# Longer score visits, an earlier first pair and fewer DMA turns in a fused cosine-attention and expert kernel

## The chip, the cores and the metric

The kernel runs on one core of a Trainium2 chip. The metric is the device time of one execution in microseconds (us); less is better. The core's engines are named as in the profile: PE (TensorE, matmuls; PEld is its weight load), ACT (ScalarE), DVE (VectorE), POOL (GpSimd) and SP (SyncE, which here only issues DMAs). ACT and POOL issue a few DMAs as well.

## The reference

For each of 8 batches and 12 heads there are q, k and v of 448 tokens by 64. The rows of q and k are divided by their norms, the scores are divided by tau = 0.1, a softmax follows, and its product with v is the attention output. The 12 heads side by side make x of 3584 tokens by 768, and two matmuls with a gate stand behind it.

```
q_n = q / (norm(q) + 1e-6);  k_n = k / (norm(k) + 1e-6)
attn = softmax(q_n @ k_n.T / tau)            # per batch and head
x = (attn @ v).transpose(0, 2, 1, 3).reshape(3584, 768)
h = x @ w_in                                 # 768 x 2048
out = (h * cos(h)) @ w_out                   # 2048 x 768
```

## The kernel before

**Names.** A pair g is two heads of one batch: there are 48 pairs, six to a batch. A unit u is three pairs (six heads, half a batch): 16 units. q, k and v of a unit are loaded as fp32 into `raw` and `vin`, which have two buffers each, used by even and by odd units. The 448 tokens are held as 4 chunks of 112. W1 is `w_in`, loaded in two halves, W2 is `w_out`, loaded in four quarters; both are fp32 in memory and bf16 on the chip, and are loaded by POOL's queue.

**The norms of a unit** (`norms`): `square` makes the squares (POOL, some on ACT or DVE), `reduce` sums them on DVE (L700), `rnorm` makes the inverse root with two ACT instructions, logarithm (L708) and exponential (L711), and `scale` multiplies, mostly on POOL (L719), into bf16 `qks`.

**Turning.** `transposes(g)` makes `qkT` of a pair. Below `BYPE` = 9 it is done by PE (L745) into the PSUM bank `PO2` (called TP there) with a copy by DVE; from pair 9 on it is a transposing DMA on SP's queue (L734).

**Scores and softmax.** `scores(g, c)` is one chunk: two matmuls (two heads, each on 64 rows of the array, side by side) into one of two PSUM buffers, SC0 and SC1 (L762), followed by one ACT exponential over 896 columns into `PX` (L767). PE goes to the scores of two chunks at a time, a "visit": `both`, called twice per pair. A score matmul uses 64 rows of the array and every other matmul the full 128, and changing from one to the other costs PE time. The planner calls this modes R and F.

**Values.** `attend(g)` is 32 small matmuls into the PSUM buffer AV (L785), then on DVE the reciprocal of the row sums (L794) and the scaling into `xs` (L795). `xs` is turned to `xT` by a DMA, or for the pairs of the first batch and the last pair of every batch by PE (L809) into the AV buffer.

**The two matmuls of a batch.** `m1(b)` is 96 matmuls (L826) in eight groups over the buffers SC0, SC1 and AV, each group followed by a cosine on ACT (L840, a sine with a shifted input) and a product on DVE (L842). ACT loads another function table before the cosines and loads the first one again after them (L618). `m2_add` and `m2_emit` make the second matmul (L877), in half tiles of 16 matmuls in `PO` and `PO2`; these are stream "B", the filler that PE takes between visits. Each half tile is copied out by DVE (L884).

**Order.** Each engine works through a fixed list in order. The lists are made when the kernel is built: operations are recorded in program order, and `arrange` plays them against listed costs and picks an order for every engine (`play`, `pick`). Up to the first `m1` PE's order is free in a window; afterwards PE takes the groups of stream "A" in order, and stream "B" between them. Gaps of the plan get dummy matmuls (L919, "filler"). In the main loop, `pair(g)` issues the first visit, `attend(g - 1)`, the DMA turn of pair g + 3 and the second visit; `m1(b)` stands after pair 12 for batch 1 and one pair into the next batch for the others (`LAG`).

Of the kernel before, what the change touches and what calls it, by code (L numbers as in the profile page):

```python
# [6 lines left out]
ACT = mybir.ActivationFunctionType  # L7
# [7 lines left out]
    "sq": ["AD", "A", "P", "P", "P", "P"],  # L15
# [4 lines left out]
DEBUG = 0  # L20
PACE, AHEAD = 0.97, 9.5
# [7 lines left out]
class Program:  # L29
# [11 lines left out]
    PATIENCE = 0.25  # L41
# [56 lines left out]
    def share(self, start, jobs, factor=1.0, first=1.2):  # L98
# [3 lines left out]
        came = {o.idx: start[o.idx] + first + (0.5 if e == "POOL" else -0.1) for e in jobs for o in jobs[e]}  # L102
# [69 lines left out]
    TRIALS = [(m, h, k) for m in ((0.0, 1.0), (0.3, 1.1), (0.8, 1.1)) for h in (0.1, 0.2) for k in (0.05, 0.2)]  # L172
# [3 lines left out]
    def arrange(self):  # L176
# [12 lines left out]
        for self.margin, self.hold, self.look in self.TRIALS:  # L189
            nominal, self.lands = first, {}  # L190
            for n in range(self.PASSES):
# [14 lines left out]
                if n:  # L206
                    spans = [self.rehearse(f, x) for f, x in self.STAGE]
                    if DEBUG:
                        print(self.margin, self.hold, self.look, n, "%.1f" % self.span, ["%.1f" % x for x in spans])
# [8 lines left out]
    def play(self):  # L218
# [45 lines left out]
        def pick():  # L264
# [4 lines left out]
            if groups and groups[0][0].free:  # L269
                for grp in groups[: self.WINDOW]:  # L270
# [3 lines left out]
                    if left[o.idx] == 0:  # L274
                        t = max(free["PE"], ready_at[o.idx])
                        if s is None or t < s - self.PATIENCE:
                            s, c = t, (t, o, grp)
                return c
            for grp in groups[:3]:
                t = when(grp)  # L280
                if t is not None and (s is None or switched(t, grp[0]) < s - self.PATIENCE):
                    s, c = switched(t, grp[0]), (t, grp[0], grp)
            if fill and left[fill[0].idx] == 0:
                o = fill[0]
                t = max(free["PE"], ready_at[o.idx])
# [16 lines left out]
        def transfer(upto):  # L302

            while clock[0] < upto:
# [10 lines left out]
                for h in run:  # L315
                    h[2] -= step * h[0].pkt / turn
                    if h[2] <= 1e-9:
                        o = queue[h[0].eng].pop(0)[0]
                        o.end = max(clock[0] + self.LAST, o.start + o.cost + 1.0)
                        if o.start > 5.0:  # L320
                            o.end += self.margin[0] + (self.margin[1] - 1.0) * (o.end - o.start)
# [8 lines left out]
        while todo or any(queue.values()):  # L330
# [23 lines left out]
            if e == "PE":  # L354
                if current:
                    current.pop(0)
                elif grp is fill:
                    fill.pop(0)
# [15 lines left out]
            if o.dma is not None:  # L374
                queue[e].append([o, o.start + (1.7 if e == "POOL" else 1.1), o.bulk + 0.02])
# [110 lines left out]
def bass_cosine_attention__then__act_gcu_kernel(  # L486
# [25 lines left out]
    BYPE = 9  # L512
# [5 lines left out]
    NO = 4  # L518
    DEFER = (2 * PB,)
# [58 lines left out]
    POv = PO.ap().bitcast(BF16)  # L578
    vav = [t.ap().rearrange("p (x d) -> p x d", d=DV) for t in va]
# [9 lines left out]
    XTv = AV.ap().bitcast(BF16)  # L589
# [48 lines left out]
    for i in range(2):  # L638
        pool(lambda e, i=i: e.memset(vav[i][:, :, D : D + 1], 1.0), (), [("va", i)], 0.15, label="ones")
# [7 lines left out]
    def load(u, p0, p1, apart=False):  # L647
        i = u % 2
        h = slice(2 * p0, 2 * p1)
        f = [lambda e, x=x, t=t: e.dma_start(  # L650
            rawv[i][:, h, NJ * x : NJ * x + NJ, :].rearrange("p h s d -> p h (s d)"), src(t, u, 2 * p0, 2 * (p1 - p0)))
            for x, t in enumerate((k, q))]
        for x in ((0,), (1,)) if apart else ((0, 1),):
            eng = "ACT" if u in HALF and x == (1,) else "SP"
            behind = quick[-1] if eng == "ACT" and quick else None if eng == "ACT" or not loads else loads[-1]
            dma(eng, [f[y] for y in x], (), [("raw", i, p, y) for p in range(p0, p1) for y in x],
                "raw%d_%d_%s%s" % (i, p0, x, eng), 0.95 * (p1 - p0) * len(x), "load u%d p%d" % (u, p0), behind, 0.068)
# [421 lines left out]
```

## Time and profile before

| | |
|---|---|
| runs | 434.74 us median of 5 (433.13 to 436.41) |
| profiled execution | 433.13 us, of which the span from first to last instruction is 431.2 us |
| granted clock of PE | 1.00 |
| PE busy | 418.1 us (97%), 3756 matmuls |
| ACT / DVE / POOL busy | 264.5 / 213.2 / 192.3 us |
| HBM | 45.61 MB read, 11.01 MB written |

The stages on PE, from its timeline (us from the start of the span): scores of batch 0 to 37, its first matmul `m1(0)` to 57, the pairs of batch 1 to 91, `m1(1)` to 109.6, then one batch after another. `m1(3)`, `m1(4)`, `m1(5)` and `m1(6)` begin at 192.5, 240.3, 288.1 and 335.8. `m1(7)` ends at 395.2, and what is left of the second matmul runs to 427.8. A line of the profile names engine, source line, operation and tiles; "idle ... <-" says what ended the engine's idle time. A filler matmul (L919) counts as busy. The width of a busy PE says little, since it is busy nearly always: the places to look at are the starts of instructions, and what stands between them.

### The profile page before, as it was taken

To read this page: it belongs to the slowest core of one execution; us is meant where nothing else is said; L and a number is where in the kernel's file an instruction comes from. 1 tells how busy PE (TensorE), PEld (TensorE's weight loads), DVE (VectorE), ACT (ScalarE), POOL (GpSimd) and SP (SyncE) were. 2 spreads that over 40 slices of the span, in tenths; PEclk is the share of its full clock that TensorE was granted. 3 is DMA by queue.
4 is the path that set the end of the run, shared out by engine and by line. 5 is a ranking of instruction groups with operands and counts; after the bars stand their busy time and mean duration, and the time that the engine had idled before them with its cause. 6 is when DMAs were issued, how large, how long until landed. Compare 5 with 4: busy or idle time off the path is not lost.

```text
span 431.2 us, 8767 instructions
## 1 busy us (share of the span) xinstructions
PE 418.1 (97%) x3756; PEld 225.7 (52%) x3756; DVE 213.2 (49%) x297; ACT 264.5 (61%) x319; POOL 192.3 (45%) x118
## 2 busy tenths in 40 slices
PE   7889989999999999999999999999999999999996
PEld 3445535554555545555555545555555545555663
DVE  5776655465636356434853375425853343344221
ACT  3887476974877647774677648774777547734000
POOL 2995248923676546932496057913596000000000
PEclk9999999999999999999999999999999999999999
DMA  8999999998179596648656692649647102200322
GB/s 218 246 242 211 241 245 199 160 249 216 33 175 248 105 273 183 114 112 239 168 117 119 164 285 62 113 128 241 149 109 133 49 0 59 59 2 2 102 79 77
DMA packets 94631, 63.87 MB, mean 148 GB/s; under 512 B 55040, under 2 KB 89600, under 8 KB 94592
## 3 DMA queue, kind: packets, MB, share of 16 engines
q1 hardware_dynamic: 90064, 56.16, 55.9%
q0 software_dynamic: 3680, 6.29, 7.9%
q10 hardware_dynamic: 848, 0.86, 0.7%
q8 instruction: 30, 0.49, 0.5%
q14 instruction: 9, 0.07, 0.1%
HBM read 45.61 MB, written 11.01 MB: 131 GB/s over the span
## 4 chain that ended last, share of the span: by engine, by line
PE 79%; DMA 7%; ACT 7%; POOL 4%; issue 1%; DVE 1%; SPq 1%; ACTq 0%
PE PO L877 26%; PE SC L826 20%; PE AV L826 12%; PE AV L785 9%; PE SC L762 8%; ACT PX L767 5%; DMA raw<-in_q_dram 4%; POOL qks L719 3%; PE SC L877 2%; DMA vin<-in_v_dram 2%; POOL sq L693 1%; DMA qkT<-qks 1%; PE AV L877 1%; ACT L618 1%; PE PO L745 0%
## 5 line engine op out<-in xcount | busy, mean ns | idle before, releaser
L767 ACT ACTIVATE PX<-SC 112x896 bf16<-112x896 f32 x192 | 164.9, 914 | 43.8 <-PE SC L762 43.4
L877 PE MATMUL PO<-W,gT 128*128 128x384 bf16 x816 | 148.6, 326 | 0.0
L693 POOL TENSOR_TENSOR sq<-raw 112x1024 bf16<-112x1024 f32 x42 | 78.9, 1895 | 99.2 <-DMA raw<-in_q_dram 99.1
L877 PEld LDWEIGHTS PO<-W,gT 128*128 128x128 bf16 x816 | 73.0, 97 | 56.9 <-issue 13.0
L719 POOL TENSOR_TENSOR qks<-raw,rn 112x1024 bf16<-112x1024 f32 x47 | 88.4, 1903 | 27.8 <-ACT rn L711 27.8
L826 PE MATMUL SC<-xT,W 128*128 128x448 bf16 x480 | 95.5, 352 | 0.3 <-ACT PX L767 0.3
L842 DVE TENSOR_TENSOR gT<-SC,cosb 128x896 bf16<-128x896 f32 x40 | 43.6, 1091 | 55.2 <-ACT cosb L840 54.7
L840 ACT ACTIVATE cosb<-SC,cst 128x896 f32<-128x896 f32 x40 | 40.2, 1007 | 48.5 <-PE SC L826 46.1
L826 PEld LDWEIGHTS SC<-xT,W 128*128 128x128 bf16 x480 | 46.6, 98 | 43.2 <-issue 0.7
L700 DVE TENSOR_REDUCE n<-sq 112x16 f32<-112x1024 bf16 (+1 forms) x49 | 58.1, 1191 | 14.6 <-POOL sq L693 9.3
L826 PE MATMUL AV<-xT,W 128*128 128x448 bf16 x288 | 58.7, 352 | 1.0 <-DVE gT L842 0.4
L762 PE MATMUL SC<-qkT 64*128 64x448 bf16 x384 | 55.3, 355 | 4.1 <-ACT PX L767 2.2
L785 PEld LDWEIGHTS AV<-va,PX 112*128 112x128 bf16 x1536 | 49.4, 97 | 15.5 <-issue 11.5
L785 PE MATMUL AV<-va,PX 112*128 112x65 bf16 x1536 | 54.7, 193 | 0.8 <-ACT PX L767 0.8
L884 DVE COPY osb<-PO 128x384 f32<-128x384 f32 x51 | 28.2, 553 | 38.0 <-PE PO L877 38.0
L840 ACT ACTIVATE cosb<-AV,cst 128x896 f32<-128x896 f32 x24 | 24.2, 1008 | 32.6 <-PE AV L826 32.4
L794 DVE RECIPROCAL rcp<-AV 112x8 f32<-112x8 f32 x48 | 9.9, 207 | 66.1 <-PE AV L785 66.1
L826 PEld LDWEIGHTS AV<-xT,W 128*128 128x128 bf16 x288 | 27.5, 98 | 28.7 <-issue 3.8
L842 DVE TENSOR_TENSOR gT<-AV,cosb 128x896 bf16<-128x896 f32 x24 | 26.2, 1091 | 19.0 <-ACT cosb L840 18.8
L795 DVE TENSOR_TENSOR xs<-AV,rcp 112x512 bf16<-112x512 f32 x48 | 33.2, 691 | 2.0
L762 PEld LDWEIGHTS SC<-qkT 64*128 64x128 bf16 x384 | 13.2, 94 | 36.5 <-ACT PX L767 17.4
L667 POOL CAST va<-vin 112x1536 bf16<-112x1536 f32 x14 | 20.5, 1466 | 10.0 <-DMA vin<-in_v_dram 7.1
(34 smaller groups left out, 122.5 us busy)
## 6 DMA issues: line engine op xcount, KB each, us to landing
vin<-in_v_dram SPq DMA_DIRECT2D x16, 672.0 KB, 9.5
raw<-in_k_dram SPq DMA_DIRECT2D x12, 672.0 KB, 8.1
raw<-in_q_dram SPq DMA_DIRECT2D x12, 672.0 KB, 10.0
W<-in_moe_w_in_dram POOLq DMA_DIRECT2D x2, 1536.0 KB, 15.6
W<-in_moe_w_out_dram POOLq DMA_DIRECT2D x4, 768.0 KB, 22.4
raw<-in_k_dram SPq DMA_DIRECT2D x12, 224.0 KB, 7.7
out_dram<-osb SPq DMA_DIRECT2D x7, 336.0 KB, 2.8
out_dram<-osb SPq DMA_DIRECT2D x8, 288.0 KB, 2.7
```

Source lines behind the costliest of these rows:

```text
L693: pool(lambda e, x=x, y=y: e.tensor_tensor(y, x, x, ALU.mult), src_, dst, 0.1 + n * 1.78e-3, label="sq%d.%d" % (u, p))
L700: dve(lambda e, w=w: e.tensor_reduce(out=n2v[i][:, 2 * p : 2 * p + 2, w], in_=sqv[p][:, :, w, :], axis=mybir.AxisListType.X, op=ALU.add), ...
L719: f = lambda e, s0=s0, s1=s1: e.tensor_tensor(qksv[i][:, p, s0:s1, :, :].rearrange("p s h d -> p h s d"), rawv[i][:, h, s0:s1, :], bass.AP ...
L762: t = e.matmul(SCv[z][:, a, 0:S], qkT[k].ap()[r, NP * c : NP * c + 128], qkT[k].ap()[r, S : 2 * S], start=True, stop=True)
L767: act(lambda e: e.activation(PXv[j][:, c, 0 : 2 * S].rearrange("p (a s) -> p a s", a=2), SCv[z][0:NP, :, 0:S], ACT.Exp, scale=1.0 / TAU), ...
L785: t = e.matmul(AVv[:, a, DV * x : DV * x + n], PXv[j][:, c, k : k + 128], vav[i][:, NJ * (2 * p + a) + c, 0:n], start=(c == 0), stop=(c == ...
L795: dve(lambda e: e.tensor_tensor(xsv[y].rearrange("p x h d -> p h x d"), AXv[:, :, :, 0:D], bass.AP(rcp[y], 0, [[NS, NP], [NJ, 2], [1, NJ], ...
L826: t = e.matmul(ph[:, a, 0:S], W1v[:, c, 128 * n : 128 * n + 128], xTv[b % 2][:, c, :], start=(c == 0), stop=(c == NKC - 1))
L840: act(lambda e, ph=ph, cz=cz: e.activation(cosv[cz], ph[:, :, 0:S], ACT.Sin, bias=cst.ap()[:, 0:1], scale=1.0), names(gi) + ["cst0"], [("c ...
L842: dve(lambda e, ph=ph, cz=cz, gi=gi: e.tensor_tensor(gTv[:, 2 * gi : 2 * gi + 2, S * (b % 2) : S * (b % 2) + S], ph[:, :, 0:S], cosv[cz], ...
L877: r = e.matmul(po[:, 0:HW], gTv[:, y, col : col + 128], W2v[:, y, HW * hf : HW * hf + HW], start=(y == 0), stop=(y == NF - 1))
L884: dve(lambda e, po=po, o=o, hf=hf: e.tensor_copy(osb[o].ap()[:, HW * hf : HW * hf + HW], po[:, 0:HW]), keys, [("osb", o, hf)], HW, label=" ...
```

## The change

1. **Three-chunk visits.** From pair `G3` = 12 on, three pairs are handled as four visits of three chunks each, where they were six visits of two. The three chunks go to the AV buffer, SC0 and SC1 in turn. So the AV buffer is shared by scores, `attend` and `m1`, and the PE turn of `xs` moves from it to `PO` or `PO2`. `m1(b)` stands after the second visit of a batch, with the first two visits' `attend` ahead of it.
2. **First pair by head.** The load of pair 0 is cut into four DMAs of one head each (two on SP, two on ACT); squares and sums of this pair are made by head, and the sums of k and q in one reduce.
3. **Early AV in four pieces.** Up to `m1(0)`, `attend` is four groups of eight matmuls that PE can place singly, where it was two of sixteen. The DVE copy of v is cut in three.
4. **Turns.** `BYPE` = 12: pairs 9 to 11 are turned by PE where they went by DMA; pairs 8 to 11 go into the AV buffer, between the visits of batch 1.
5. **W1.** Both halves are issued by POOL right behind the square of pair 2, one after the other. Before, the first waited for v of unit 0, and the second stood seven POOL instructions later, ahead of W2.
6. **Other moves.** The squares of pair 3 go from POOL to ACT; unit 2 gets its norms as two pairs and one, and its last square goes from ACT to POOL. The load of unit 5 waits in order for the turn of pair 12. The second matmul's half tiles are kept and spread by `KEEP` and `SPREAD`, so that a part of each batch stands right behind `m1`. The planner's listed costs for DMAs and its trial settings are other ones.

```diff
-    "sq": ["AD", "A", "P", "P", "P", "P"],
+    "sq": ["AD", "A", "P", "A", "P", "P"],
...
-    BYPE = 9
+    BYPE = 12
+    GATE = "T12"
+    BEHIND = "sq0.2"
+    G3 = 12
+    KEEP = (0, 1, 0, 1, 0, 1, 0)
+    SPREAD = (5, 6, 6, 6, 6, 6, 6)
+    AT, AT1 = 1, 1
...
     def load(u, p0, p1, apart=False):
+        if u == 0 and p0 == 0:
+            for a in range(2):
+                for x, t in enumerate((k, q)):
+                    eng, past = ("SP", loads) if x == 0 else ("ACT", quick)
+                    dma(eng, [...src(t, u, a, 1)], (), [("raw", i, 0, x, a)], ...)
...
+        if g >= PB + UP - 1:
+            views, keys = (AVt, AVt), ("AV", "AV")
...
     def scores(g, c):
-        j, k, z = g % 2, g % UH, (c + 1) % 2
+        j, k, q = g % 2, g % UH, NJ * g + c
+        name, bank = PHs[1 + (c + 1) % 2 if g < G3 else q % 3]
...
+        step = 1 if P.free else 2
+        for x0 in range(0, NJ, step):
+            P.op("PE", lambda e, x0=x0: av(e, x0, step), ...)
...
+        keys, view = ["PO"], POv
+        if g >= 2 * PB - 1:
+            keys, view = [(["PO"], POv), ([("TP", 0), ("TP", 1)], TPv)][nhalf[0] % 2]
...
+    def visit(g, n):
+        q = NJ * g + 3 * n
+        for x in range(q, q + 3):
+            scores(x // NJ, x % NJ)
...
+    def project(b, g):
+        m1(b)
+        if g in DEFER:
+            norms(g // UP + 1, 0)
+            for x in range(g + 3, g + 4 + AT1):
+                transposes(x)
+        ...                      # loads of units 2b + 4 and 2b + 5, after m1's first matmul
+        m2_add(b)
+        m2_emit(SPREAD[b])
...
     load_w1(0)
-    after(P.ops[-1], find("load v u0"))
     load_w1(1)
...
+    P.order_only(find("sq0.2"), find("W1.0"))
+    P.order_only(find(BEHIND), find("W1.1"))
...
-    for g in range(PB, NG):
-        pair(g)
-        if g in points:
-            m1(points[g])
-            ...
+    for g in range(G3, NG, 3):
+        for n in range(4):
+            if n < 3:
+                ahead(g + n)
+            grouped(visit, g, n)
+            if n < 3 and g + n > PB:
+                attend(g + n - 1)
+            if n == 0:
+                values(g)
+            if g % PB == 0 and g > PB and n == (AT if g > 2 * PB else AT1):
+                project(g // PB - 1, g)
```

## The prediction

> **What bounds the kernel now.** I read the page first, then the table by stage, the timeline of one steady batch, the chain, and the DMA queues of the early stage. The table's columns are the stretch, its length, then busy us and number of instructions for PE, PEld, DVE, ACT and POOL, PE's clock, DMA share and GB/s.
>
> ```profile
> PE 418.1 (97%) x3756; PEld 225.7 (52%) x3756; DVE 213.2 (49%) x297; ACT 264.5 (61%) x319; POOL 192.3 (45%) x118
> ```
>
> ```profile
> 57.00:91.10 34.10, 32.32 (x355) 17.39 (x355) 18.02 (x27) 28.16 (x36) 26.16 (x15) 1.00 1.04 202
> ...
> 240.30:288.10 47.80, 47.69 (x442) 25.59 (x441) 24.73 (x34) 32.18 (x39) 25.32 (x14) 1.00 0.64 154
> ```
>
> PE is the bound, at full clock, from 109 us on; no other engine passes 70% of a steady batch (second row). In the first row (pairs of batch 1) ACT is at 28.2 of 34.1 us and the DMA engines are full: that stage is a near tie. One steady pair in PE's timeline, then the ACT and DVE of the same pair:
>
> ```profile
> 215.69 2.12 PE L877 MATMUL PO<-W,gT 128*128 128x384 bf16 x12
> 217.74 0.55 PE L762 MATMUL SC<-qkT 64*128 64x448 bf16 x4
> 218.23 1.14 PE L785 MATMUL AV<-va,PX 112*128 112x65 bf16 x32
> 219.20 0.81 PE L877 MATMUL PO<-W,gT 128*128 128x384 bf16 x4
> 219.95 0.55 PE L762 MATMUL SC<-qkT 64*128 64x448 bf16 x4
> ```
>
> ```profile
> 218.15 1.73 ACT L767 ACTIVATE PX<-SC 112x896 bf16<-112x896 f32 x2 [0.78 <-PE SC L762]
> ...
> 219.40 0.21 DVE L794 RECIPROCAL rcp<-AV 112x8 f32<-112x8 f32 x1 [2.22 <-PE AV L785]
> ...
> 219.64 0.69 DVE L795 TENSOR_TENSOR xs<-AV,rcp 112x512 bf16<-112x512 f32 x1
> ```
>
> Read starts, not ends. In the chain, 24 matmuls of m1 take 4.54 us (at 192.69), 0.189 each, and in the tail 32 of the second matmul take 5.20, 0.1625 each. A visit of two chunks lasts from 217.74 to 218.23 = 0.49; two chunks are 0.38, so leaving the 64-row mode costs 0.11. Twelve L877 matmuls are 1.95, but 215.69 to 217.74 is 2.05: entering costs 0.10. **A visit costs 0.21 us beside its work.** The 32 AV matmuls take 0.97. A steady batch is then 96 x 0.189 + 0.27 (one wait for DVE in m1) + 100 x 0.1625 + 12 x (0.38 + 0.21) + 6 x 0.97 + 0.2 (the turn L809) = 47.7; from m1(4) to m1(5) it is 47.8. Nothing else is in it.
>
> The chain that ended last:
>
> ```profile
> 57.45 1.01 ACT cosb L840
> 58.48 1.28 ACT L618
> 59.77 2.54 ACT PX L767 x3
> ...
> 70.06 5.30 DMA qkT<-qks
> ...
> 156.62 1.90 POOL sq L693
> ...
> 420.04 5.20 PE SC L877 x32
> ```
>
> Early it is ACT, not PE: exponentials to 35.9, last cosine and table to 59.77; then one turn that sits 5.3 us behind loads on SP. From 192.69 on it is PE without a break.
>
> **The change part by part.** The sum is made against the profiled execution (span 431.2, time 433.13; the 1.9 us around the span stay). That run is the fastest of the five: the median lies 1.6 above, and I carry the difference over to it.
>
> *Three-chunk visits.* The built order of the changed kernel shows them from pair 12 on. From m1(1) to the end there were 69 visits of two chunks and are 46 of three (34.5 pairs both times). Saved: 23 x 0.21 = **4.8**.
>
> What this adds is a wait. Before, 12 filler matmuls or a whole visit lay between the last exponential of a pair and its AV. The new order is visit, 4 or 8 L877, AV, and the AV needs a chunk of the visit just made. The first exponential starts 0.41 after its visit (217.74 to 218.15), takes 0.914 (page, L767), a second follows 0.82 later (1.73 for two), and PE sees the end some 0.05 later (in the early rows a score started at 11.15, the exponential before it ended at 11.10). A three-chunk visit lasts 3 x 0.189 + 0.11 = 0.67.
> - First and second AV of three: visit and 4 matmuls, 1.32, against 0.41 + 0.91 + 0.05 = 1.37: wait 0.05.
> - Third: second chunk needed, 0.67 + 1.30 = 1.97 against 2.19: wait 0.22.
> - Last pair: third chunk, 2.62 against 3.01: 0.4.
>
> Per three pairs 0.32; 35 AVs are left: 11.7 x 0.32 + 0.4 = **4.1 given back**. Here a rule speaks harder: the Trainium skill, "TensorEngine Tiling (Array Packing)", section "PSUM Bottleneck", says that tiling the array speeds up the matmuls but not the emptying of PSUM, which may then be the bound. Taken whole (each AV waits for the visit's three exponentials, 3.01 after its start) the cost is some 1.7 a pair on two AVs of three and 1.0 on the third, over 50 in all. By the rows only the chunk that the AV reads counts, and ACT has 15 us free per batch; I take the rows.
>
> The AV buffer is now handed from AV to DVE to the next visit. L794 starts 0.20 after the AV matmuls and L795 ends 1.13 after them; 8 L877 and the entry are 1.40. Hidden, by 0.2 us. A sum L700 (1.2 us, page) in front of L794 on DVE would uncover up to 1.2. In the built DVE order the sums stand in m1 or ahead of an AV with 2 us of room. Cost 0, bounds 0 and +0.1 per AV (3.5). After m1, 16 L877 (2.6) cover cosine and product (2.3): 0.
>
> *A stall that goes.* From m1(2) to m1(3) took 48.67, 0.9 over a steady batch: the load of unit 8 was issued behind two turns (4.0 us on SP), its square ran at 156.62, and m1's product waited for the sum. In the built order the load precedes those turns. **-0.9**; bounds 0 and -0.9.
>
> *First pair by head.* Four DMAs for two add 0.45 us of issue on SP and ACT; halves are squared while the rest lands. Gain about 0.25 at the first score (9.77). But ACT idles 1.93 ahead of pair 1 (exponential at 16.33), which POOL sets. So 0, and a later landing of up to 1.9 is covered too.
>
> *W1 and POOL.* POOL waited 0.83 for v ahead of W1; now W1's second issue (0.9) stands there: pair 1 is scaled at 12.5 as before. Later POOL is ahead: the square of pair 3 fills ACT's idle 1.9, and pair 5 is scaled about 1.1 earlier. ACT idled 0.61, 0.79 and 0.40 in 24 to 33; I take 1.2 of these 1.8. With them early AV in four pieces; its cover is the same ACT chain, and the two more DVE copies of v (some 0.2 each) lie in idle DVE. m1(0) starts near 35.8 (before 37.05).
>
> *That lead is lost at the end of m1(0).* ACT gets the square of unit 3's last pair between the last two cosines, and it waits for that load; table, unit 2's last norm and all exponentials of batch 1 queue behind. The queues while W1 ran (622 and 620 packets, 18 to 26 us):
>
> ```profile
> q0 software_dynamic: 622, 1.27, 83.7%
> q1 hardware_dynamic: 620, 0.59, 27.5%
> ```
>
> In these 8 us W1 moves 159 GB/s, the loads 74. Both halves now run back to back, from 16.9 (0.9 earlier than before, with the issue) to 37 us; unit 2 lands around 40 (before 33.3), unit 3 follows at 97 GB/s (the loads' 0.97 MB in 44 to 54 us, beside W2): 1.376 MB take 14.2, and the last queues come 1.5 later: 56.2 (before 58.1). The square ends at 57.3, the last cosine at 58.3, table and norm at 59.9: the same as 59.77. Lead lost, **0**; bounds -1.5 and +3.
>
> *Batch 1.* PE gets four turns more there (8 x 0.05 each, 1.6; m1(0) one less, 0.4) and one AV more (0.97). Gone are the 2.9 behind the late DMA turn (ACT idle 2.92 ahead of 75.8) and fillers. Work 33.3 against 30.9, waits 2 against 3.2. m1(1) starts at 91.0 (before 91.1) **-0.1**, and the AV done early is gone from the rest: **-1.0**.
>
> Sum: -4.8 + 4.1 - 0.9 - 0.1 - 1.0 = -2.7. Span 428.5; at the median 434.74 - 2.7 = **432.0**.
>
> **The rivals.**
> 1. *The waits stay small and the lead is kept.* Unit 3 lands by 54.5, and most AV waits vanish since ACT runs ahead. For: DMA is never idle; 15 us of ACT free per batch. Against: the 1.97 and 2.19 above. Another -1.2 and up to -3: about 428.
> 2. *Slower: the square in front of the last cosine.* W1's second half before unit 2 and 3 is the price, one place: the load of unit 3. Each us it lands after 56.2 delays the table and the exponentials of batch 1 one for one, in a stage where ACT has 28.2 of 34.1 us. Break-even with the -2.7 is a landing at 58.9, 0.8 later than the row of before. At 61: +2.2, 437.
> 3. *Nothing left.* DVE comes 0.08 late to each of 35 handoffs: +2.8, 434.8.
>
> That the change does not do what it says is excluded by the built order.
>
> **How the numbers follow.** Likeliest (0.46): 432.0, its own range 430.2 to 433.6. Rival 1: 0.22. Rival 2: 0.17. Rival 3: 0.15. About 0.5% (2.2 us) is what a measurement of this kernel can tell from no change, so faster means under 432.6: three quarters of the likeliest and rival 1, 0.56. Slower: rival 2 and a little of 3, 0.19. The rest 0.25. Range 427.5 to 437.5, leaving out a tenth on each side.
>
> **What would show it.** Right: starts of visits of 0.67; AV waits for ACT of 0.05 and 0.2; batches of about 49.5 us with 112 L877 in each; 144 L877 after m1(7), not 200; m1(1) near 91; first exponential of batch 1 near 60. Wrong: PE idle ended by L795 ahead of a score into AV (rival 3), a square on ACT ended by a DMA after 58 us (rival 2), AVs with no wait (rival 1), a new wait for a turn on SP ahead of a visit.

## The result, and the profile after

| | before | after |
|---|---|---|
| runs | 435.05 us median of 80, the five of the first table among them (432.65 to 438.42) | 434.54 us median of 43 (432.66 to 438.43) |
| ratio, 95% interval | | 0.9993 (0.9982 to 1.0004) |
| profiled execution, its span | 433.13, 431.2 | 434.53, 432.7 |
| granted clock in it | 1.00 | 0.992 |

No change that can be measured; 432.0 had been forecast. On another chip, with fresh runs of both, the ratio was 1.0027 (1.0007 to 1.0047, that is 0.3 to 2.0 us slower). So the forecast gain of 2.7 us is on neither chip. The two intervals do not overlap: the same two kernels can differ by 0.3% more or less from chip to chip. The page after:

```profile
PE 418.9 (97%) x3773; PEld 229.0 (53%) x3773; DVE 214.3 (50%) x305; ACT 263.0 (61%) x322; POOL 192.2 (44%) x118
...
PEclk9799999999999999999999999999999999999999
```

PE is as busy as before, with 17 matmuls more. New is the 7 in the second slice: the clock was cut there. The table by stage (columns as in the prediction), the pairs of batch 1 and one steady batch:

```profile
60.00:92.50 32.50, 31.90 (x402) 18.37 (x400) 17.52 (x29) 27.58 (x38) 22.58 (x14) 1.00 0.61 156
...
242.70:292.00 49.30, 49.07 (x448) 26.70 (x444) 24.83 (x34) 31.49 (x39) 25.33 (x14) 1.00 0.60 149
```

The second `m1` begins at 92.53 (before 91.12, forecast 91.0). A steady visit in PE's timeline:

```profile
263.87 0.36 PE L791 MATMUL AV<-qkT 64*128 64x448 bf16 x2
264.07 0.54 PE L791 MATMUL SC<-qkT 64*128 64x448 bf16 x4
264.54 1.47 PE L911 MATMUL PO<-W,gT 128*128 128x384 bf16 x8
266.05 1.14 PE L814 MATMUL AV<-va,PX 112*128 112x65 bf16 x32
267.03 1.46 PE L911 MATMUL PO<-W,gT 128*128 128x384 bf16 x8
268.43 0.36 PE L791 MATMUL AV<-qkT 64*128 64x448 bf16 x2
```

The visit is 263.87 to 264.54 = 0.67, as worked out. The eight L911 after it take 1.51, which is 8 x 0.1625 and a wait of 0.21 for the exponential; ahead of the other AVs four take 0.70, a wait of 0.05. Steady batches take 49.56 and 49.59 (from 193.19, 242.75 and 292.34). So the visits and their waits (0.05 and 0.21, worked out as 0.05 and 0.22) are as forecast.

The chain of the early stage shows where the first microsecond stands:

```profile
12.32 26.22 DMA W<-in_moe_w_in_dram
...
38.91 18.39 DMA raw<-in_q_dram
57.33 0.26 ACT sq L711
57.59 0.70 issue
58.29 0.99 ACT cosb L877
59.30 1.28 ACT L628
60.59 0.31 ACT lnn L730
60.90 0.80 ACT PX L796
```

W1's second half lands at 38.5. The load of unit 3 is ordered behind it and lands at 57.3, the square of its last pair stands on ACT ahead of the last cosine, and the first exponential of batch 1 comes at 60.80 on ACT's timeline (the chain counts it from the end of the logarithm, 60.90; before 59.77). And POOL and PE at the start:

```profile
9.46 1.89 POOL L715 TENSOR_TENSOR sq<-raw 112x1024 bf16<-112x1024 f32 x1 [7.99 <-DMA raw<-in_q_dram]
...
11.30 1.84 POOL L944 DMA_DIRECT2D W<-in_moe_w_in_dram  x2
...
13.16 3.77 POOL L741 TENSOR_TENSOR qks<-raw,rn 112x1024 bf16<-112x1024 f32 x2
...
15.12 0.57 PE L773 MATMUL PO<-ident,qks 112*128 112x112 bf16 x8 [2.17 <-POOL qks L741]
```

Pair 1 is scaled at 13.16 (forecast 12.5) and PE pauses 2.17 us for it. The next view, by stretches of 4 us (the eighth figure group, ahead of the DMA share, is PE's clock), has the consequence:

```profile
16.00:20.00 4.00, 3.85 (x40) 1.71 (x37) 3.23 (x6) 2.49 (x4) 4.00 (x3) 0.59 1.13 243
20.00:24.00 4.00, 4.00 (x45) 2.16 (x43) 2.14 (x3) 3.39 (x7) 3.33 (x4) 0.56 1.11 233
```

The clock is at half from 16.7 to 23.5. Of the 44 executions listed of this kernel (the 43 and the profiled one) 37 have a mean clock of 0.996 or less, of 43 of the kernel before on the other chip 3; the medians of after go with it: 434.24 us at 1.00, 434.68 at 0.996, 434.75 at 0.992, 435.26 at 0.988.

Later PE waits twice for DVE, once ahead of a turn of `xs` and once ahead of a visit, in the timeline at 138 and at 317:

```profile
138.05 1.22 DVE L721 TENSOR_REDUCE n<-sq 112x16 f32<-112x1024 bf16 x1 [0.17 <-POOL sq L715]
...
139.19 0.20 DVE L824 RECIPROCAL rcp<-AV 112x8 f32<-112x8 f32 x1
...
140.17 0.37 PE L844 MATMUL PO<-ident,xs 112*128 112x112 bf16 x4 [0.62 <-DVE xs L825]
```

```profile
316.93 1.22 DVE L721 TENSOR_REDUCE n<-sq 112x16 f32<-112x1024 bf16 x1 [0.17 <-POOL sq L715]
318.06 0.20 DVE L824 RECIPROCAL rcp<-AV 112x8 f32<-112x8 f32 x1
...
319.04 0.36 PE L791 MATMUL AV<-qkT 64*128 64x448 bf16 x2 [0.74 <-DVE xs L825]
```

A sum of a unit whose load was late stands ahead of the reciprocal that empties the AV buffer, and what PE does next needs that division or that buffer: 0.62 and 0.74 us are lost.

To compare batches with unlike contents I took from each one's length its own matmuls (96 x 0.189 for `m1`, 0.1625 for each L911, 0.19 for each chunk, 0.0305 for each AV matmul, 0.049 for each turn). What is left, us from the start of each `m1` to the next; the last column is the sum from `m1(1)` to PE's end, with the two shorter stages that follow `m1(6)`:

| kernel | m1(1) | m1(2) | m1(3) | m1(4) | m1(5) | sum |
|---|---|---|---|---|---|---|
| before, first trace (433.13) | 3.4 | 3.0 | 2.8 | 2.8 | 2.8 | 16.8 |
| before, second trace (435.22) | 4.3 | 3.7 | 2.8 | 3.8 | 2.8 | 19.4 |
| after, first trace (434.53) | 4.0 | 2.7 | 2.6 | 2.6 | 3.6 | 18.2 |
| after, second trace (433.36) | 3.6 | 2.7 | 2.6 | 2.6 | 2.6 | 16.7 |
| two-chunk form of after | 3.6 | 3.3 | 2.8 | 2.9 | 2.9 | 17.6 |
| before, short loads | 3.2 | 2.5 | 2.8 | 2.8 | 2.8 | 16.1 |
| after, short loads | 3.2 | 2.6 | 2.6 | 2.6 | 2.6 | 16.3 |
| two-chunk form, short loads | 3.4 | 3.3 | 2.8 | 2.9 | 2.9 | 17.3 |
| after, W1 put back | 4.6 | 2.6 | 2.6 | 2.6 | 2.6 | 17.2 |

### The profile page after: what moved, and what is told of

Read it like the earlier page. It is cut to its first block, busy times and chain, and to the rows that moved or that the text cites. A ratio compares the mean times of both kernels' runs of the same rounds, so it can differ in the third digit from the quotient of the medians.

```text
span 432.7 us, 8824 instructions
## 1 busy us (share of the span) xinstructions
PE 418.9 (97%) x3773; PEld 229.0 (53%) x3773; DVE 214.3 (50%) x305; ACT 263.0 (61%) x322; POOL 192.2 (44%) x118
## 4 chain that ended last, share of the span: by engine, by line
PE 71%; DMA 19%; POOL 3%; ACT 2%; SPq 2%; DVE 1%; issue 1%; ACTq 0%; DVEq 0%; POOLq 0%
PE PO L911 29%; PE SC L863 13%; DMA raw<-in_q_dram 11%; PE AV L814 9%; PE AV L863 9%; DMA W<-in_moe_w_in_dram 6%; PE SC L791 5%; PE AV L791 3%; POOL sq L715 2%; ACT PX L796 2%; PE AV L911 1%; PE SC L911 1%; DMA vin<-in_v_dram 1%; SPq L669 1%; POOL qks L741 1%
## 5 line engine op out<-in xcount | busy, mean ns | idle before, releaser
L911 PE MATMUL PO<-W,gT 128*128 128x384 bf16 x832 | 152.0, 327 | 0.1
L796 ACT ACTIVATE PX<-SC 112x896 bf16<-112x896 f32 x144 | 123.9, 916 | 8.0 <-PE SC L791 7.8
L911 PEld LDWEIGHTS PO<-W,gT 128*128 128x128 bf16 x832 | 74.3, 98 | 62.9 <-issue 18.4
L741 POOL TENSOR_TENSOR qks<-raw,rn 112x1024 bf16<-112x1024 f32 x47 | 88.3, 1903 | 16.9 <-ACT rn L733 16.7
L796 ACT ACTIVATE PX<-AV 112x896 bf16<-112x896 f32 x48 | 44.0, 917 | 49.8 <-PE AV L791 49.8
L877 ACT ACTIVATE cosb<-SC,cst 128x896 f32<-128x896 f32 x40 | 40.2, 1007 | 46.7 <-PE SC L863 43.8
L814 PE MATMUL AV<-va,PX 112*128 112x65 bf16 x1536 | 55.7, 194 | 0.8 <-ACT PX L796 0.3
L791 PE MATMUL SC<-qkT 64*128 64x448 bf16 x288 | 42.9, 361 | 2.6 <-DVE qkT L781 1.1
L877 ACT ACTIVATE cosb<-AV,cst 128x896 f32<-128x896 f32 x24 | 24.2, 1006 | 28.6 <-PE AV L863 28.5
L879 DVE TENSOR_TENSOR gT<-AV,cosb 128x896 bf16<-128x896 f32 x24 | 26.2, 1090 | 16.1 <-ACT cosb L877 16.0
## 6 DMA issues: line engine op xcount, KB each, us to landing
out_dram<-osb SPq DMA_DIRECT2D x7, 336.0 KB, 3.1
```

The lines of the kernel that those rows point to most:

```text
L741: f = lambda e, s0=s0, s1=s1: e.tensor_tensor(qksv[i][:, p, s0:s1, :, :].rearrange("p s h d -> p h s d"), rawv[i][:, h, s0:s1, :], bass.AP ...
L791: t = e.matmul(bank[:, a, 0:S], qkT[k].ap()[r, NP * c : NP * c + 128], qkT[k].ap()[r, S : 2 * S], start=True, stop=True)
L796: act(lambda e: e.activation(PXv[j][:, c, 0 : 2 * S].rearrange("p (a s) -> p a s", a=2), bank[0:NP, :, 0:S], ACT.Exp, scale=1.0 / TAU), [n ...
L814: t = e.matmul(AVv[:, a, DV * x : DV * x + n], PXv[j][:, c, k : k + 128], vav[i][:, NJ * (2 * p + a) + c, 0:n], start=(c == 0), stop=(c == ...
L877: act(lambda e, ph=ph, cz=cz: e.activation(cosv[cz], ph[:, :, 0:S], ACT.Sin, bias=cst.ap()[:, 0:1], scale=1.0), names(gi) + ["cst0"], [("c ...
L879: dve(lambda e, ph=ph, cz=cz, gi=gi: e.tensor_tensor(gTv[:, 2 * gi : 2 * gi + 2, S * (b % 2) : S * (b % 2) + S], ph[:, :, 0:S], cosv[cz], ...
```

## The experiments

All ratios are to the kernel before, measured beside the run. Runs 1 to 4 share a chip, and so do 5 to 7, 8 and 9, 10 and 11, and the two of 12. The changed kernel itself ran only for the result and in run 5, so what another run gains over it is known no better than to the 0.3% above. In runs 1, 2, 3 and 7 one instruction or a few were moved in the finished lists, so that every other instruction kept its order (`move(a, b)` puts a right behind b); run 9 and the first kernel of 12 do the same with the lists of 6 and 10. Runs 6, 10, 11 and the second kernel of 12 were planned anew. Labels: `sq`, `red`, `ln`, `rn`, `scale` with unit and pair; `sin0.7` is the last cosine of `m1(0)`, `xs17` the division of pair 17.

**1. The last cosine ahead of unit 3's square.**

```diff
     P.arrange()
+    move("sq3.2", "exp6.0")
+    move("red3.2", "red3.1")
```

> Only the square of unit 3's last pair (on ACT) and its sum (on DVE) change place: behind the second exponential of batch 1, instead of ahead of the last cosine of the first m1. Every other instruction keeps its order. Theory A (the time lost early is ACT's wait for the load of unit 3, which lands at 57.3): the last cosine starts where the first m1 ends, 57.5 instead of 58.29, the first exponential of batch 1 near 60.1 instead of 60.90, the second m1 starts 0.8 earlier (91.7 instead of 92.53), and the whole is 0.8 us faster than the changed kernel: 433.7. Rival B (batch 1 is bounded by PE and its own waits): the first exponential is earlier, the second m1 is not, 434.5.

Measured: 433.61 us, ratio 1.0002 (0.9984 to 1.0019). By the ratio that is no gain over before, and none over after that can be told. In the trace the first exponential of batch 1 came at 58.41, 2.4 us earlier, but the second `m1` at 91.27, 1.3 earlier, and a part of this is not the move's: unit 3 landed at 56.8, 0.5 earlier. The chain names the next in line:

```profile
56.89 3.74 POOL sq L715 x2
60.63 1.87 POOL qks L741
...
62.55 0.57 PE AV L773 x8
```

Pair 8's scaling stands on POOL behind two squares that wait for the same load. Unit 3's landing holds batch 1 by two ways, and freeing one gives a part of the stage.

**2. The late sums behind the division.**

```diff
+    move("red7.2", "xs17")
+    move("ln7.0", "exp18.3")
+    move("rn7.0", "exp18.3", 0.002)
+    move("scale7.1", "rn7.0")
+    move("red15.1", "xs37")
```

> Only the sums L721 that stood on DVE between an AV and its reciprocal in the trace of the changed kernel (at 138.05 and at 316.93) are moved behind that AV's division; the logarithm and norm of the first one follow behind one exponential. Everything else keeps its order. Theory A (each of these two sums holds the AV buffer, and so the next visit, by 0.7 to 0.8): both waits go, the stretch from the second to the third m1 is 49.6 instead of 50.3, that from the sixth to the seventh 49.7 instead of 50.55, the whole is 1.5 us faster: 433.0. Rival B (units 7 and 15 are late, so another wait takes the place): at most 0.3 faster, 434.3.

Measured: 434.27 us, ratio 1.0009 (0.9995 to 1.0023): rival B. The wait at 138 was gone (the eight L911 there took 1.30), and the third `m1` lost 1.3 us instead. The chain behind it:

```profile
143.25 5.63 POOL qks L741 x3
...
149.04 0.58 SPq L669
...
149.66 7.68 DMA raw<-in_q_dram
...
157.41 1.90 POOL sq L715
...
159.33 0.04 DVE n L721
...
160.47 1.09 DVE gT L879
```

The later sum made unit 7's scaling later, with it the turn on SP, with it the load of unit 8 that stands behind that turn, its square, its sum, and the product of `m1` that stands behind the sum. Nothing in this row is slow; each is a list that is worked in order.

**3. W1's second issue behind pair 1's scaling.**

```diff
+    move("W1.1", "scale0.1")
```

> Only the second issue of W1 on POOL moves behind the scaling of pair 1. Everything else keeps its order. Theory A (the second issue delays pair 1, and the pause of PE that follows halves its clock, but unit 3's landing hides all that): pair 1 is scaled at 12.3 instead of 13.16, the granted clock stays at 1.0 from 15 to 24 us, the first m1 starts at about 37.0 instead of 37.95, and the last cosine and the whole stay: 434.0 to 434.5. Rival B (the late start of the first m1 passes through to the end): 433.6.

Measured: 433.99 us, ratio 1.0016 (0.9999 to 1.0032). PE's pause was 1.46, the clock stayed at 1.0 from 15 to 24 us, `m1(0)` began at 36.43 (37.95), and the first exponential of batch 1 at 60.97. Theory A: the early lead does not get past unit 3's landing (57.47 here). It even cost something there: PE was done with what it could do at 59.2, waited for the product behind the last cosine, and after that wait its clock was cut (the 0.50 in the second view), so that the second `m1` began at 93.67.

```profile
60.94 0.81 PE L911 MATMUL PO<-W,gT 128*128 128x384 bf16 x4 [1.70 <-DVE gT L879]
```

```profile
62.60:66.00 3.40, 3.40 (x19) 1.43 (x17) 1.54 (x3) 3.08 (x6) 3.39 (x3) 0.50 0.17 34
```

**4. Six fillers in the pause.**

```diff
+        for n in range(6):
+            o = self.op("PE", fns["PO"], cost=took, mode="F", label="filler")
+            o.deps, o.start = [(zero, True)], 12.9 + 0.02 * n
```

> Six filler matmuls more (448 columns, 1.1 us together) on PE in its pause ahead of pair 1's turns, at about 13 us; nothing else changes. Theory A (the pause of 2.2 us is what halves the clock, from 16.8 to 23.5): the clock stays at 1.0 in this stretch, the first m1 starts 0.3 to 0.9 earlier, the whole 0 to 0.5 faster: 434.3. Rival B (another, earlier pause or the share of PE's work as a whole sets the clock): it still drops, nothing changes.

Measured: 434.73 us, ratio 1.0029 (1.0005 to 1.0052); in the trace the pause was 0.70, and by stretches:

```profile
16.00:20.00 4.00, 3.20 (x35) 1.41 (x31) 3.90 (x7) 3.15 (x5) 4.00 (x3) 1.00 1.13 240
20.00:24.00 4.00, 3.21 (x53) 2.03 (x54) 2.85 (x5) 4.00 (x9) 3.65 (x4) 1.00 1.10 231
```

The pause is what cuts the clock: with dummy work in it alone, 5 of 14 executions have a mean clock of 0.996 or less, where 37 of 44 had in after, and 11 of 14 in run 1 on this chip. In the trace `m1(0)` began at 36.35 and ended at 56.23 (57.54), but the first exponential of batch 1 came at 60.76 and the second `m1` at 92.48 (92.53): the lead buys nothing there, and the time did not get better.

**5. A second trace of both.**

> The changed kernel as it is, beside the others of this call, for a second trace and a time on the same chip. If the stages differ from run to run only ahead of the second m1, its steady batches last 49.5 to 49.6 again and the start of the second m1 moves within 91.3 to 94.2. Theory (late loads hold back sums and squares that stand in front of others): stalls sit at the same places as in the first trace, with other sizes.

> The kernel before as it is, for a second trace. Theory A (the first trace of before was one of its fast runs, by its early stage): the second m1 starts later than 91.12, at 92 to 93, and from there to the end of PE it takes 336.7 again. Rival B (the early stage of the kernel before is steady): the second m1 starts at 91.1 again, and the difference lies later.

Measured: after 434.85 us, ratio 1.0027 (1.0007 to 1.0047); its second `m1` began at 92.94 and the batches from the fourth `m1` on were steady. Before, one execution of 435.22: its second `m1` began at 90.69, earlier than in the first trace, but from there it took 339.3 to PE's end instead of 336.7. Rival B: the early stage of before is steady, and its first trace was one with few stalls behind it. By this second pair of traces after is 1.9 us faster (433.36 to 435.22), by the first 1.4 slower: single executions differ by more than the change is worth. In both pairs after is later at the second `m1`, by 1.4 and 2.25.

**6. Visits of two chunks.**

```diff
-    G3 = 12
+    G3 = NG
+    points = {PB * (b + 1) + (0 if b == 1 else LAG): b for b in range(1, B - 1)}
...
         grouped(both, g, 2)
+        if g in points:
+            project(points[g], g)
```

> The changed kernel with visits of two chunks to the end, in the two score buffers, as before; its early stage, loads and turns by PE are those of the changed kernel. Theory A (three-chunk visits save 4.8 and give 4.1 back, and two sums ahead of the buffer's handoff cost up to 1.5 of the rest): within 0.7 of the changed kernel, to either side; a steady batch with 112 second-matmul groups of four would take 49.7 instead of 49.55. Rival B (the sharing of the AV buffer is what ate the gain): the two-chunk form is faster than the changed kernel by more than 1 us. Rival C (the visits carried a gain that the early stage eats): slower than the changed kernel by 2 or more.

Measured: 433.73 us, ratio 0.9983 (0.9965 to 1.0001), 1.1 us faster than after (434.85) on the same chip: rival B at the median, though the two profiled executions were equal (433.44 and 433.36) and the table shows 0.2 to 0.3 more per batch for two chunks. The two-chunk runs lie closer together (the middle half within 0.5 us, of after within 0.8).

**7. All the waits at once.**

```diff
+    move("sq3.2", "exp6.0")
+    move("red3.2", "red3.1")
+    move("rn2.2", "ln2.2")
+    find("scale2.2").eng = "DVE"
+    move("scale2.2", "red3.0")
+    ...                          # red7.2, ln7.0, rn7.0, scale7.1, red15.1 as in 2
+    move("red8.0", "g2.5")
+    move("red8.1", "g2.6")
+    move("red8.2", "g2.7")
```

with the fillers of 4.

> The changed kernel with work taken from in front of those who waited, every other instruction in its order: the square of unit 3's last pair behind the second exponential of batch 1; the norm of pair 8 ahead of the first exponential and its scaling on DVE instead of POOL (where it stood behind two squares that wait for unit 3); the sums of units 7 and 15 behind the division; the sums of unit 8 behind the products of m1; six filler matmuls more at 13 us. Theory A (the gain is lost at these waits for loads): the first exponential of batch 1 at 59.7 or earlier, pair 8 turned by 61.6 instead of 63.84, the second m1 at 90.5 instead of 92.53, no stall at 138 nor in the third m1; 2.8 us faster than the changed kernel, ratio to before near 0.993. Rival B (each wait only hands over to the next late load, as the turns of unit 7 and the load of unit 8 did): less than 1 us faster, ratio 0.997 or more.

Measured: 434.68 us, ratio 1.0007 (0.9992 to 1.0023), 0.2 us faster than after: rival B. The first exponential came at 58.86, but pair 8's turn was copied out only at 64.63, behind unit 3's sums on DVE, and the second `m1` began at 92.43. In the third `m1` unit 8's logarithm then stood on ACT, ahead of the exponentials, for the sum that I had moved.

**8. Short loads.** Units 4 to 15 load 16 of 112 rows, in three kernels; the other rows keep older data, so these kernels are for timing alone.

```diff
-        return bass.AP(..., [[NJ * D, NP], [S * D, nh], [1, NJ * D]])
+        return bass.AP(..., [[NJ * D, NP if u < 4 else 16], [S * D, nh], [1, NJ * D]])
```

> The changed kernel, in which the loads of units 4 to 15 bring 16 of the 112 rows only (the rest of those buffers keeps older data): their transfers are short, every instruction and its order stay. Units 0 to 3, W1 and W2 are loaded in full, so the early stage stays. Theory A (from the second m1 on the gain is eaten by sums and norms that wait for late loads and stand ahead of handoffs): the stalls go, every batch from the second m1 on takes its steady length (112 groups of the second matmul: 49.5), the runs spread less, and the kernel is 0.5 to 0.7 faster than the two-chunk form with the same short loads. Rival B (the shared AV buffer costs more than worked out, late loads or not): it is slower than that form by 1 us, as it was with full loads (434.85 against 433.73).

> The two-chunk form of the changed kernel, with the same short loads of units 4 to 15 (16 of 112 rows). Theory A: a batch with 112 groups takes 49.8 to the end, its stalls (0.5 in the third m1) go, and it gains less from the short loads than the three-chunk form. Rival B: it gains as much, and stays 1 us ahead.

> The kernel before, with the same short loads of units 4 to 15 (16 of 112 rows). Theory A: the stalls that its second trace showed (0.9, 0.7 and 1.0 us in three batches) go, it gains 1.5 to 2.5 us at the median and spreads less; the changed kernel with short loads then stands against it by the budget alone: between 0.8 faster and 0.3 slower. Rival B: it gains as much as the changed kernel or more.

Measured: after 432.98 us, ratio 0.9978 (0.9961 to 0.9995); two-chunk form 434.26, 0.9997 (0.9978 to 1.0016); before 431.94, 0.9955 (0.9938 to 0.9971). Theory A for the visits: with loads that are never late, three chunks are 1.3 us faster than two, where they were 1.1 slower with full loads; late loads eat what the visits give. But before gains 2.0 us as well and stands 1.0 ahead of after, which theory A did not expect: late loads are a cost of both kernels, and not what keeps after from being faster. With short loads nothing is left to explain that behind the second `m1` (16.1 and 16.3 in the table): it lies in the early stage. Before's second `m1` began at 91.03, after's at 94.28. Of these 3.25 us, 1.35 are work moved ahead (one AV, two chunks of scores), and a part is the clock, which was at half for 10.2 us in this trace of after.

**9. The two-chunk form with the cosine first and the fillers** (edits of 1, 4 and 6).

> The two-chunk form of the changed kernel with full loads, with the square of unit 3's last pair and its sum behind the second exponential of batch 1, and six filler matmuls more at 13 us. Theory A (of the early stage, the wait of the last cosine for unit 3 and the halved clock are what can be had): the first exponential of batch 1 comes at 58.5 to 59 instead of 60.7, the second m1 at 89.5 instead of 90.77, and the kernel is 1.2 faster than the two-chunk form: 432.5, ratio to before 0.9955. Rival B (pair 8's scaling behind unit 3's squares on POOL takes the place): the second m1 at 90.5, 433.5.

Measured: 433.49 us, ratio 0.9979 (0.9962 to 0.9995). First exponential at 59.25, second `m1` at 90.97 (90.77 without): rival B by the numbers. What its trace shows is another wait than the one named there: PE stood 1.54 us, until 61.39, for the landing of a part of W2 that the second matmul needed, with pair 8's scaling (from 61.17 on) close behind.

**10. W1's second half and unit 2's norm as before.**

```diff
-            square(u, x, "A" if u in (3, 4, 5) and x == 2 else "P")
+            square(u, x, "A" if u in (2, 3, 4, 5) and x == 2 else "P")
...
-    P.order_only(find(BEHIND), find("W1.1"))
+    P.order_only(find("scale1.1"), find("W1.1"))
...
-    norms(2, 0, UP - 1)
+    norms(2, 0)
...
-    for g in range(PB, PB + UP - 1):
+    for g in range(PB, PB + UP):
         transposes(g)
...
-    norms(2, UP - 1)
```

> The changed kernel with one part undone: the second half of W1 is issued behind the scaling of unit 1's second pair again (near 24 us instead of 12), and all of unit 2 is normed and turned ahead of and in the first m1, as before. First pair by head, AV in four pieces, turns by PE and three-chunk visits stay. Theory A (W1's second half queued right behind the first closes the hole in which unit 2 came in: its last load lands at 41.2 instead of 33.3, and pair 8's norm and scaling fall behind the first m1 and behind unit 3's squares): unit 2 lands near 34 again, pair 8 is turned in the first m1, the second m1 starts at 91.0 to 91.5 instead of 92.5 to 92.9, the kernel is 1 to 1.5 us faster than the changed one: ratio to before near 0.998. Rival B (batch 1 is bound by unit 3's landing through the last cosine, whatever the place of W1's half): the second m1 at 92.5, ratio 1.001.

Measured: 433.61 us, ratio **0.9973** (0.9957 to 0.9989): theory A, and faster than before, as it is again with one more change in run 12 (0.9982, on another chip). Against after the ratios speak for it too (0.9993 and 1.0027), but after did not run beside it. The second `m1` began at 92.13 (92.53 and 92.94), not as early as expected, and the batch behind it carried 4.6. The queues from 28 to 31 us, packets, MB and share of the 16 engines, after and then this kernel:

```profile
q0 software_dynamic: 235, 0.48, 83.9%
q1 hardware_dynamic: 233, 0.22, 27.5%
```

```profile
q0 software_dynamic: 168, 0.34, 60.2%
q1 hardware_dynamic: 414, 0.39, 54.2%
```

Between the two halves of W1 the loads get nearly twice as much through. Unit 2's last load is complete at 31.96, where it was 41.2; and W1's second half, issued at 25.34 instead of 12.32, lands at 38.44, where it landed at 38.54. Issuing it 13 us earlier had brought W1 nothing. Unit 3 landed at 57.61, no earlier than in after (57.30). Unit 2 is now scaled ahead of and in `m1(0)`; POOL after, and here:

```profile
61.88 1.90 POOL L741 TENSOR_TENSOR qks<-raw,rn 112x1024 bf16<-112x1024 f32 x1 [0.77 <-ACT rn L733]
```

```profile
37.96 5.62 POOL L741 TENSOR_TENSOR qks<-raw,rn 112x1024 bf16<-112x1024 f32 x3 [3.04 <-ACT rn L733]
```

The scaling at 61.88, which held pair 8, is one of the three at 37.96. The square on ACT now stands behind the first exponentials, too, which came at 60.23. How the gain is shared between W1's place, unit 2's norm and the newly planned lists is not shown.

**11. The whole early part as before** (10, and: first pair's load, squares and sums, AV in two pieces, `BYPE` = 9, the first wait of W1, the planner's two DMA costs).

> The late part of the change alone: loads of the first pair, squares, W1, unit 2's norm, AV pieces and the turns of pairs 9 to 11 as in the kernel before; three-chunk visits from pair 12 on, the AV buffer shared, loads ahead of turns, as in the changed kernel. Theory A (the early part of the change costs about 1 to 2 us by W1's order and the halved clock, and the late part alone is worth what the budget gives, less the stalls): the clock stays at 1.0, unit 2 lands near 33, the second m1 starts at 92.3 to 92.8 with one AV and a visit more ahead of it (before: 90.7 to 91.1, plus 1.55), and the kernel stands between 0.5 faster and 0.5 slower than before: 0.999 to 1.001. Rival B (the early part is not what costs): as the changed kernel or slower, 1.002 or more.

Measured: 436.80 us, ratio 1.0059 (1.0033 to 1.0085): rival B by the number, but the plan was another one, so it does not price the early part. What it does show is the turn of pair 9 by DMA, in its chain:

```profile
68.05 6.47 DMA qkT<-qks
...
74.57 0.57 PE SC L791 x4
```

6.5 us behind loads, as it was 5.3 in the kernel before. This speaks for the turns by PE, though no run tests them alone.

**12. Two steps on from 10**: unit 7's sum moved as in 2, and the two-chunk form as in 6.

```diff
+    move("red7.2", "xs17")
+    move("ln7.0", "exp18.3")
+    move("rn7.0", "exp18.3", 0.002)
+    move("scale7.0", "rn7.0")
```

> The changed kernel with W1's second half and unit 2's norm back as before, and the last sum of unit 7 behind the division of the AV it stood ahead of, its logarithm and norm behind one exponential more; all else in the order of the run before with W1 put back. Theory A (that sum's 1.2 us are the 1.4 us stall at 138 and nothing takes their place): the batch from the second m1 takes 49.6 instead of 50.9, the next stays at 49.53, 1.3 us faster than with W1 put back alone: ratio to before near 0.994. Rival B (the delay is handed on through the scaling of unit 7 and the load of unit 8): the next batch gets longer by as much, ratio 0.997.

> The changed kernel with W1's second half and unit 2's norm back as before, and visits of two chunks to the end in the two score buffers. Theory A (late loads now hurt the three-chunk form in one place only): the two forms stand within 0.5 us, ratio to before 0.996 to 0.998. Rival B (three-chunk visits gain 1.3 us as they did with short loads): 0.9995 or more. Rival C (the two-chunk form is immune and stays 1 us ahead, as it was in the changed kernel): 0.995 or less.

Measured: 432.93 us, ratio 0.9982 (0.9966 to 0.9998), and 436.09, 1.0068 (1.0042 to 1.0094). In the first the two batches carry 4.3 and 3.5 where they carried 4.6 and 2.6: handed on again, rival B. In the second another list came out, whose batch behind the second `m1` carries 7.0 (some 1.7 of them from a stretch of 3.4 us at half clock; the trace is of the slowest execution, 440.69); none of the three cases had that, and it does not settle which form is better with W1 put back.

## Why the prediction was wrong

The step that failed is batch 1, "m1(1) starts at 91.0 (before 91.1) -0.1". The second `m1` began at 92.53 and 92.94 in the two traces of after, at 91.12 and 90.69 in those of before: 1.4 and 2.25 us later. Behind it a gain of 2.6 was forecast (-4.8 + 4.1 - 0.9 - 1.0). From the second `m1` to PE's end before took 336.7, 339.3 and, with short loads, 336.0; after took 336.8, 335.2 and 334.8. Without late loads that is a gain of 1.2, all of it work moved ahead into batch 1 (1.35), and the early stage takes it back and more. What else had been forecast there is missing by two steps below: the stall of 0.9, of which 0.65 was work, and fillers of 0.65 that had no term.

By its own steps, in the first pair of profiled executions (span forecast 428.5, measured 432.7: 4.2 to account for):

- **Visit overhead and three-chunk visits: right.** Visits of 0.67, waits of 0.05 and 0.21 for the exponential, steady batches of 49.56 and 49.59, 144 L877 (now L911) behind the last `m1`. A steady batch carries 2.6 beside its work against 2.8; the net of -4.8 and +4.1 is 0.12 a batch. The rows, not the rule of the Trainium skill ("TensorEngine Tiling (Array Packing)", section "PSUM Bottleneck") taken whole, were the ones to follow: not 50 us but 4. A small slip: before had 70 visits there (35 pairs), not 69.
- **Handoff of the AV buffer at 0: the mechanism named, the size wrong.** The text gave 1.2 us for a sum in front of the reciprocal, and took 0 since the built order showed room. The order holds only as long as loads land when the list assumes. Two such sums cost 0.62 and 0.74 in this trace. Against the kernel with short loads after carries 1.9 more (18.2 to 16.3), before 0.7 (16.8 to 16.1): 1.2 of the 4.2. In the second traces it is 0.4 and 3.3, so this term is the luck of a single execution; run 8 shows late loads as a cost of both kernels.
- **Stall of 0.9 that goes: wrong by 0.65.** The stage from `m1(2)` had 104 second-matmul instructions, the steady ones 100, and 4 x 0.1625 is 0.65: work, not a wait. Only 0.25 was over the steady length. Nor did the load precede the turns: SP's timeline after has two of them ahead of it.

```profile
142.84 3.35 SPq L760 DMA_TRANSPOSE qkT<-qks  x2
146.23 0.58 SPq L669 DMA_DIRECT2D raw<-in_k_dram  x1
```

- **A supply that ran out: not foreseen.** In the batch from `m1(1)` one AV has two fillers ahead of it (0.70 with a short wait) instead of four L911, because 108 are left there. That is the 0.65 by which that batch exceeds the steady ones with short loads (3.2 to 2.6).
- **First pair by head at 0: right that it is hidden, wrong that it is free.** The first score came 1.04 earlier (8.73), not 0.25. But the load of pair 2 landed 0.74 later (9.32), its square started 0.74 later on POOL, and both W1 issues stand behind it.
- **W1 and POOL: the lead was wrong, and did not matter; the price of unit 2 did.** "Pair 1 is scaled at 12.5 as before": 13.16. "`m1(0)` starts near 35.8": 37.95 with the clock at half and 37.09 at full clock, after pauses of 2.17 and 2.14. But runs 3 and 4, which had the lead (36.43 and 36.35), began the second `m1` no earlier. Unit 2 "around 40" was right (41.2), but its price was set at nothing: pair 8 is normed behind `m1(0)` and scaled behind unit 3's squares, which held batch 1 in run 1. Run 10 undoes this and is faster than before.
- **Batch 1 at -0.1: the failed step.** Having given up the lead of 1.2, the text counts 33.3 of work and 2 of waits from an end of `m1(0)` at 55.7, which has the lead in it. Run 4 shows that this end is not the point to count from: 56.23 there, 57.54 in after, and the same second `m1`. The first exponential is. It was put at 59.9 and came at 60.80, because unit 3 landed at 57.3 and not at 56.2. From it to the second `m1` the forecast leaves 31.1, and it took 31.7; two chunks of scores more (0.38) had no term. These 0.9 and 0.6 are the 1.5 at the second `m1`.
- **AV done early, -1.0: right.** 1120 AV matmuls follow the second `m1`, 1152 did.

1.5 at the second `m1`, 0.65 for the stall that was work, 0.65 for the fillers and 1.2 for late loads are 4.0 of the 4.2. This is the account of one pair of executions; in the second pair after is 1.9 faster, which is chance as well.

Rival 2's place was the right one, the square ahead of the last cosine, and the first exponential followed the landing as it said, though this came at 57.3 and not beyond 58.9. Its reason was not: in the kernel before unit 3 landed at 58.1, later than after, with the first exponential at 59.77. The place of the square made the landing count, and W1's second half delayed unit 2, not unit 3. Rival 3's small lateness at each handoff is not there: the cost came in a few large pieces.

Not settled: what the first pair by head, the squares and the AV pieces each cost by themselves (run 11 came with another plan), how the early loss at the median is shared between the square's place, pair 8 and the clock, and whether three or two chunks are better once W1 is put back.

## What to carry to other kernels

Before a difference between two stages is called a stall, take each one's own matmuls from its length: two thirds of the 0.9 here were four instructions more. In lists that are worked in order, an instruction that waits for a load must not stand ahead of one that frees a buffer or ends a stage, and moving it only helps if what depends on it has room as well; several of the runs here only handed the wait on. A lead that ends at a wait for a load is worth nothing behind it. And an earlier issue behind another transfer of its queue need not bring earlier data (38.54 us for an issue at 12.3, 38.44 for one at 25.3), but it can close the gap in which others came through (unit 2 at 41.2 and not at 32.0).

## What the hardware showed that I had not expected

PE's clock went to half after a pause of 2.17 us at about 13 to 15 us; pauses of 1.91, 2.42, 2.64, 2.71 and 3.03 at that place in other runs had the same result, and so had one of 1.70 (run 3) and one of 2.25 (run 12) later on. Pauses of 0.64 to 1.61 left it at full, and once one of 2.14 did. The mean clocks of whole executions come in steps (1.00, 0.996, 0.992, 0.988), each some 3.4 us at half clock; in the traces the stretches at half last 3.4, 6.8 or 10.2 us.

The Trainium skill ("TensorE: Matmul & The Clock Gate", section "Part 1: The HAM clock gate") has windows of about 3.4 us that run on by themselves, and half clock after an idle one. Counted off in steps of 3.41 us from the clock's changes in each trace, such windows sort the cases better than the pauses do. In eight of nine drops the window just ahead had 1.72 to 2.59 us, of its 3.41, without a matmul on PE (1.85 here); behind the first microseconds, no window with 1.61 or less was followed by a drop but one. The pause of 2.14 fell into two windows, with 0.96 and 1.39 us idle. So a window did not have to be idle as a whole, and where a pause falls decides. The exception is run 6: its pause of 1.76 fell into two windows, with 0.96 and 1.12 us idle, and the drop at 20.75 came behind the next one, with 1.15; it stays unexplained.

A stage in which PE is not the bound can lose its lead in this way: `m1(0)` began at 37.95 in the first trace of after, at 37.09 in the second, with as long a pause but full clock, and at 36.35 in run 4, with neither.
